# An S4 convolution and attention stack: the weights split in the first stage, and the first block of rows turned before the convolution has ended

## The chip, the cores and the metric

The kernel runs on one core of a Trainium2 chip. The metric is the device time of one execution in microseconds. Besides plain times there is one profiled execution, with a trace of every engine: TensorE (PE, with its weight loads as PEld), VectorE (DVE), ScalarE (ACT), GpSimd (POOL), SyncE (SP) and the DMA queues.

## The reference

Four layers with a residual each, over x of 2048 rows by 640 columns in float32: convolution "a", attention "b", convolution "c", attention "d". Both convolutions use the same parameters, and both attentions the same weights.

```python
def _A_ref(u, A_re, A_im, B_re, B_im, C_re, C_im, log_dt, Dskip):
    ...
    P = jnp.exp(logdA[:, :, None] * l[None, None, :])
    K = jnp.einsum("dn,dnl,dn->dl", Cc, P, dB).real
    ...
    y = irfft(rfft(pad(u)) * rfft(pad(K)))[..., :L] + u * Dskip
def _B_ref(x, wq, wk, wv, wo):
    q, k, v = heads(x @ wq), x @ wk, x @ wv      # 32 heads of 20, one k and one v
    return softmax(q @ k.T * 20 ** -0.5) @ v @ wo
x = A_u
x = x + _A_ref(_layernorm(x), ...)
x = x + _B_ref(_layernorm(x), ...)
x = x + _A_ref(_layernorm(x), ...)
x = x + _B_ref(_layernorm(x), ...)
```

## The kernel before

The stages stand one behind the other. First `kgen` makes the convolution kernel K (0 to about 340 us). `kg_tables` works out small tables on DVE and ACT; each table is cut into three bf16 parts (`cast`, `rest`), written to DRAM and read back in another layout by `send` and `send_late` into `ta`, `tb` and `tm`, all on SP's queue. Then 20 units follow: phases (`phase`, PE from `tb` and `ta`), sines (`trig`, ACT), sizes (`sizes`, PE from `tm`), exponentials, products on DVE, sums on PE. `store` puts a unit's result into the staging tile `kst`, and after each eighth unit, and after the last, `kst` goes to DRAM as `kd`. Of the load of x (`load_x`, eight DMAs) the statistics need the result from unit 5 on.

`kernel_spectra` loads `kd` back (four chunks `kts`, the fifth `ktl`, on POOL's queue) and makes the spectra `kh` of the five chunks of 128 columns. `conv_layer` then goes over the five chunks c: product with `kh`, an 8-point transform woven with other calls (`weave` puts a call at a given place between DVE instructions), and the inverse on PE for four groups g of rows, each in a PSUM bank. `residual` adds a group's result to the stream `self.x`; `turn(g)` does that and starts the inverse of group g + 2. In chunk 3 the stream itself goes through PE by an identity matmul, so that ACT only copies. Behind the last chunk stand the statistics of the rows (`stats_last`, `norm_part`).

For the attention the weights wq, wk, wv are needed as a rounded part `wh` and a rest `wl`. In layer "a" `attn_weights` makes them: six pieces, each with a copy on ACT, matmuls with the identity and its negative on PE (tile `pw`), a second copy on ACT; the pieces are woven into the last chunk's product, and both results are written to DRAM (`whd`, `wld`). In layer "c" they are only read back. `_attn` begins with `prepare(0)`: ACT normalises the first 512 rows, PE transposes them (20 transposes into tile `ptb` or `ptd`), ACT makes the rounded part `xh`, DVE the rest `xl`. Then the projections of block 0 start (tiles `pqb`, `pqd`, L1001).

On PE, ACT and DVE the order in these stages is that of the code (`manual_schedule`); in `kg_tables` also that of SP. A DMA or POOL instruction goes where the Tile framework puts it. Where pools are laid out in memory decides which tile shares its bytes with which earlier one, and a load into such bytes waits until the earlier tile's last reader is done.

Of the kernel before, what the change touches and what calls it, by code (L numbers as in the profile page):

```python
# [21 lines left out]
P = 128  # L22
# [120 lines left out]
class Net:  # L143
# [7 lines left out]
    def setup(self, ctx):  # L151
        tc, nc = self.tc, self.nc
        self.cp = ctx.enter_context(tc.tile_pool(name="cp", bufs=1))
        self.dr = ctx.enter_context(tc.tile_pool(name="dr", bufs=1, space=DRAM))
        self.ident = self.cp.tile([P, P], F32, name="ident")
        self.halfpi = self.cp.tile([P, 1], F32, name="halfpi")
        nc.vector.memset(self.halfpi, 0.5 * math.pi)
        self.xp = ctx.enter_context(tc.tile_pool(name="xp", bufs=1))
        self.x = self.xp.tile([P, 16, D], F32, name="x")
        self.mv = self.xp.tile([P, 16, 2], F32, name="mv")  # L160
        self.kd = self.dr.tile([NCH, P, 16 * DC], F32, name="kd")
        self.kh = self.dr.tile([NCH, P, 32 * DC], F32, name="kh")
# [26 lines left out]
    def kg_tables(self, pp, hs, t3, SH, ldt, aim, are_raw, bre, bim, cre, cim, ta, tb, tm):  # L189
# [49 lines left out]
        V(mn, ar, ai, ALU.min)  # L239
        T(mx, mx, 1e-37, None, ALU.max)  # L240
# [31 lines left out]
        A(u3, u2, AF.Ln, bias=1.0)  # L272
        nc.vector.tensor_copy(hs["ph"][:, 0], ph)
# [406 lines left out]
    def load_spectrum(self, c):  # L680
        A = self.cvp.tile([P, 16, 256], F32, tag="kh", bufs=2, name=f"kh{c}")
        self.nc.sync.dma_start(A.rearrange("p s d -> p (s d)"), self.kh[c])
        return A

    def kernel_spectra(self):

        nc, cv = self.nc, self.cvp

        kts = cv.tile([P, 4, 16, DC], F32, tag="wi", name="kts")
        ktl = cv.tile([P, 24, DC], F32, tag="xn", name="ktl")  # L690
        ks = [kts[:, c] for c in range(4)] + [ktl[:, 0:16]]
        dsk = ktl[0:1, 16:21]
        nc.gpsimd.dma_start(dsk.rearrange("p c d -> p (c d)"), self.ins["A_Dskip"][None, :])
        for c in range(NCH):
            nc.gpsimd.dma_start(ks[c].rearrange("p t d -> p (t d)"), self.kd[c])

        def skip(c):
            k = ks[c][0:1, 0]
            nc.vector.tensor_tensor(k, k, dsk[:, c], ALU.add)

        skip(0)
        Z = {0: self.raw(ks[0], "k0")}
        for c in range(NCH):
            if c + 1 < NCH:
                skip(c + 1)
                Z[c + 1] = self.raw(ks[c + 1], f"k{c + 1}")
            A = cv.tile([P, 16, 256], F32, tag="kh", bufs=2, name=f"kn{c}")
            weave(self.radix(Z.pop(c), A) + fft8(nc, A, self.B, self.R, -1), ())
            nc.sync.dma_start(self.kh[c], A.rearrange("p s d -> p (s d)"))

    def conv_layer(self, nm, first):
# [6 lines left out]
        with tc.manual_schedule(engines={mybir.EngineType.PE, mybir.EngineType.Activation,  # L718
# [25 lines left out]
            def new_xn(c):  # L744
                return cv.tile([P, 24, DC], F32, tag="xn", bufs=1, name=f"xn{nm}{c}")
# [18 lines left out]
            def inverse(c, g, A):  # L764
                y = self.ps1(f"y{nm}{c}{g}")
                v = A.rearrange("p s (k d) -> p s k d", k=2)
                whole = c == NCH - 2
                if whole:
                    nc.tensor.matmul(y, self.ident, stream(c, g), start=True, stop=False)
# [37 lines left out]
            for c in range(NCH):  # L807
                A = As.pop(c)
                mul = product(A, khs.pop(c)) + fft8(nc, A, B, R, +1)
                if c == NCH - 1:  # L810
                    late = sorted(late + [(1 + k, a[0]) for k, a in enumerate(pieces)]
                                  + [(3 + k, a[1]) for k, a in enumerate(pieces)], key=lambda a: a[0])
# [35 lines left out]
        turn(0)  # L848
        self.stats_base()
        self.norm_part(0, 1)  # L850
        for g in range(1, 4):
            turn(g)
        self.norm_part(1, 3)

    def attn_setup(self):
# [4 lines left out]
        self.whd = dr.tile([P, 5 * 692], F32, name="whd")  # L860
        self.wld = dr.tile([P, 5 * 692], F32, name="wld")
# [9 lines left out]
    def attn_weights(self, scr, fresh):  # L871


        nc, ins = self.nc, self.ins
        stack = ExitStack()
# [4 lines left out]
        parts = [(w.bitcast(F32), dst) for w, dst in ((wh, self.whd), (wl, self.wld))]  # L880
        if not fresh:
            for w, dst in parts:
                nc.sync.dma_start(w, dst.rearrange("p (k n) -> p k n", k=5))
            return []
        kv = wp.tile([P, 5, 52], F32, name="kv")
        nc.gpsimd.memset(kv, 0.0)
        nc.sync.dma_start(kv[:, :, 0:20], ins["B_wv"].rearrange("(k p) n -> p k n", p=P))
        nc.sync.dma_start(kv[:, :, 32:52], ins["B_wk"].rearrange("(k p) n -> p k n", p=P))
        minus = scr[:, 2816:2944]
        nc.scalar.activation(minus, self.ident, AF.Copy, scale=-1.0)  # L890
        pws = {}

        def ends(k):
            return (wh[:, k - 1, 0:D], wl[:, k - 1, 0:D]) if k else (wh[:, :, D:692], wl[:, :, D:692])

        def first(k):
            hi = ends(k)[0]
            pw = pws[k] = self.ps2(f"pw{k}")
            if k:
                src = scr[:, D * (k % 2) : D * (k % 2) + D]  # L900
                nc.sync.dma_start(src, ins["B_wq"][P * (k - 1) : P * k])
                cuts = [(pw[:, a:b], src[:, a:b], hi[:, a:b]) for a, b in ((0, 512), (512, D))]
            else:
                src = kv
                cuts = [(pw[:, 0:260].rearrange("p (k n) -> p k n", k=5), src, hi)]
            nc.scalar.activation(hi, src, AF.Copy)
            for o, a, _ in cuts:
                nc.tensor.matmul(o, self.ident, a, start=True, stop=False)
            for o, _, b in cuts:
                nc.tensor.matmul(o, minus, b.bitcast(F32), start=False, stop=True)  # L910

        def second(k):
            pw = pws.pop(k)
            src = pw[:, 0:D] if k else pw[:, 0:260].rearrange("p (k n) -> p k n", k=5)
            nc.scalar.activation(ends(k)[1], src, AF.Copy)
            if k == 5:
                for w, dst in parts:
                    nc.sync.dma_start(dst.rearrange("p (k n) -> p k n", k=5), w)

        return [(lambda k=k: first(k), lambda k=k: second(k)) for k in range(6)]  # L920
# [19 lines left out]
    def _attn(self, ctx, nm, out):  # L940
# [20 lines left out]
        with tc.tile_pool(name=f"pj{nm}", bufs=1, reuse_waits="tile") as pj:  # L961
# [5 lines left out]
            xhs, xls = {}, {}  # L967

            def prepare(nb):

                xs = []
                for i in range(4):
                    t = 4 * nb + i
                    x = pj.tile([P, D], F32, tag="x", bufs=4, name=f"x{nb}{i}")
                    nc.scalar.activation(x, self.x[:, TAUS[t]], AF.Identity, scale=self.rs[:, t : t + 1],
                                         bias=self.nmr[:, t : t + 1])
                    xs.append(x)
                xh = xhs[nb] = pj.tile([P, 5, 512], F32R, tag="xh", bufs=2, name=f"xh{nb}")
                xl = xls[nb] = pj.tile([P, 5, 512], F32R, tag="xl", bufs=2, name=f"xl{nb}")
                for k0, n in ((0, 2), (2, 2), (4, 1)):  # L980
                    pt = self.ps2(f"pt{nm}{nb}{k0}")
                    for k in range(n):
                        for i in range(4):
                            nc.tensor.transpose(pt[:, 512 * k + 128 * i : 512 * k + 128 * i + 128],
                                                xs[i][:, 128 * (k0 + k) : 128 * (k0 + k) + 128], self.ident)
                    self.split(xh[:, k0 : k0 + n], xl[:, k0 : k0 + n],
                               pt[:, 0 : 512 * n].rearrange("p (k c) -> p k c", k=n), act=True)

            def project(nb):
                cols = slice(512 * nb, 512 * nb + 512)  # L990
                xh, xl = xhs.pop(nb), xls.pop(nb)
                pn = None
                late = []
                for m in (5, 0, 1, 2, 3, 4):
# [13 lines left out]
                    if m == 1 and nb < 3:  # L1008
                        prepare(nb + 1)
# [32 lines left out]
            prepare(0)  # L1042
# [290 lines left out]
```

## Time and profile before

| | us |
|---|---|
| median of 3 runs (lowest, highest) | 3069.56 (3068.69, 3069.82) |
| profiled execution | 3071.17 |
| its span, first to last instruction | 3069.4 |
| PE busy in it | 2874.8 (94%) |
| ACT busy | 2428.3 (79%) |
| DVE busy | 1404.4 (46%) |
| POOL busy | 41.5 (1%) |

A row of the timeline gives a start, a duration, the engine, the line of the program, the operation with its tiles (out<-in), how many instructions of the kind follow one another (xN), and in brackets how long the engine had been idle before and what ended that. A row of a window gives the busy time of each engine in a stretch, the granted clock of PE, the share of time in which the DMA engines were busy, and GB/s.

### The profile page before, as it was taken

How to read it: one execution, taken by the hardware profiler on the slowest of the kernel's cores; microseconds unless marked ns; L12 is line 12 of the kernel's file. 1: busy time of each engine (PE TensorE's matmuls, PEld its weight loads, DVE VectorE, ACT ScalarE, POOL GpSimd, SP SyncE). 2: the span in 40 equal slices, each digit the busy share in tenths (PEclk: the TensorE clock that was granted, in tenths of full speed). 3: DMA queues.
4: the chain of work that ended last, by engine and by line, in shares of the span. 5: the costliest groups of instructions: out<-in, count | busy, mean ns of one | idle time of the engine just before them, and what ended most of it. 6: DMA issues, size and time to landing. Idle time of an engine off the chain costs nothing. (4 is left out here: it accounts for less than half of the span.)

```text
span 3069.4 us, 52317 instructions
## 1 busy us (share of the span) xinstructions
PE 2874.8 (94%) x21696; PEld 1362.8 (44%) x21696; DVE 1404.4 (46%) x1793; ACT 2428.3 (79%) x2910; POOL 41.5 (1%) x113
## 2 busy tenths in 40 slices
PE   2888898989899999999999989798999999999999
PEld 0555887867323323333233479673223333333233
DVE  7888799972122232232222399922122222222223
ACT  5777343353899999999999633446999999999997
POOL 0000000000100000000000000000000000000000
PEclk9999999989999999999999999899999999999999
DMA  6010551123300010000100210132000100100100
GB/s 143 18 29 17 177 220 56 38 83 131 112 24 25 22 28 22 24 25 22 27 23 24 112 55 28 50 125 79 23 22 25 39 27 24 39 25 21 45 19 22
DMA packets 72177, 158.82 MB, mean 52 GB/s; under 512 B 21509, under 2 KB 27653, under 8 KB 67797
## 3 DMA queue, kind: packets, MB, share of 16 engines
q1 hardware_dynamic: 65880, 137.70, 14.9%
q0 software_dynamic: 4080, 16.67, 1.5%
q8 instruction: 175, 2.87, 0.4%
q10 hardware_dynamic: 1968, 0.98, 0.1%
q14 instruction: 74, 0.60, 0.1%
HBM read 95.22 MB, written 48.04 MB: 47 GB/s over the span
## 5 line engine op out<-in xcount | busy, mean ns | idle before, releaser
L1134 ACT ACTIVATE pt<-scb 128x1024 f32<-128x1024 f32 x1024 | 942.2, 1115 | 7.5 <-PE scb L1130 5.8
L1134 ACT ACTIVATE pt<-scd 128x1024 f32<-128x1024 f32 x1024 | 942.2, 1118 | 7.0 <-PE scd L1130 5.5
L1144 PE MATMUL pod<-pt,vt 128*32 128x512 f32 x4096 | 546.9, 606 | 4.4 <-DVE on L1161 0.8
L1144 PE MATMUL pob<-pt,vt 128*32 128x512 f32 x4096 | 546.9, 606 | 4.3
L1130 PE MATMUL scb<-qpb,kt 62*128 62x512 f32 x2048 | 386.0, 451 | 6.2 <-PEq L1079 5.8
L1130 PE MATMUL scd<-qpd,kt 62*128 62x512 f32 x2048 | 385.8, 451 | 5.8 <-PEq L1079 5.5
L1130 PEld LDWEIGHTS scd<-qpd,kt 62*128 62x128 f32 x2048 | 166.1, 185 | 402.0 <-ACT pt L1134 392.3
L1130 PEld LDWEIGHTS scb<-qpb,kt 62*128 62x128 f32 x2048 | 165.9, 185 | 402.1 <-ACT pt L1134 392.6
L1192 DVE TENSOR_TENSOR x<-pyd,x 128x320 f32<-128x320 f32 x146 | 71.7, 491 | 561.0 <-PE pyd L1204 561.0
L1192 DVE TENSOR_TENSOR x<-pyb,x 128x320 f32<-128x320 f32 x146 | 71.7, 491 | 547.7 <-PE pyb L1204 547.7
L1164 DVE RECIPROCAL rc<-rc 128x512 f32<-128x512 f32 x62 | 207.9, 3353 | 2.1
L1144 PEld LDWEIGHTS pob<-pt,vt 128*32 128x32 f32 x4096 | 80.7, 108 | 178.3 <-issue 160.3
L1144 PEld LDWEIGHTS pod<-pt,vt 128*32 128x32 f32 x4096 | 80.6, 108 | 177.7 <-issue 159.7
L421 PE MATMUL pk<-s,m 128*64 128x32 f32 x1280 | 130.8, 295 | 13.3 <-DVE s L412 13.3
L421 PE MATMUL pk<-c,e1r 128*64 128x32 f32 x1280 | 132.1, 297 | 11.4 <-DVE c L411 11.2
L421 PEld LDWEIGHTS pk<-c,e1r 128*64 128x64 f32 x1280 | 105.3, 221 | 79.6 <-issue 52.2
L579 PE MATMUL za<-xna,wf 128*128 128x256 f32 x512 | 113.0, 383 | 2.7 <-ACT xna L733 2.7
L421 PEld LDWEIGHTS pk<-s,m 128*64 128x64 f32 x1280 | 108.1, 226 | 15.9 <-DVE s L412 15.9
L579 PE MATMUL zc<-xnc,wf 128*128 128x256 f32 x512 | 111.5, 379 | 2.7 <-ACT xnc L733 2.7
L581 ACT ACTIVATE Aa<-za 128x1024 f32<-128x1024 f32 x16 | 16.4, 1023 | 118.3 <-PE za L579 116.9
L581 ACT ACTIVATE Ac<-zc 128x1024 f32<-128x1024 f32 x16 | 16.4, 1024 | 113.7 <-PE zc L579 113.7
L579 PEld LDWEIGHTS za<-xna,wf 128*128 128x128 f32 x512 | 98.0, 192 | 16.7 <-ACT xna L733 3.3
(308 smaller groups left out, 3272.9 us busy)
## 6 DMA issues: line engine op xcount, KB each, us to landing
kh<-kh SPq DMA_DIRECT2D x10, 2048.0 KB
kh<-kn SPq DMA_DIRECT2D x5, 2048.0 KB
qhd<-qh SPq DMA_DIRECT2D x40, 256.0 KB
qld<-ql SPq DMA_DIRECT2D x40, 256.0 KB
qpb<-qhd SPq DMA_DIRECT2D x256, 40.0 KB
qpd<-qhd SPq DMA_DIRECT2D x256, 40.0 KB
ot<-on SPq DMA_DIRECT2D x216, 40.0 KB
wf<-in_c_wf POOLq DMA_DIRECT2D x16, 512.0 KB, 7.9
```

What stands on the lines that cost most here:

```text
L421: nc.tensor.matmul(PK[u][64 * par : 64 * par + 64, 32 * d : 32 * d + 32], e[u][:, d, par], c[u][:, d, par], start=first, stop=not first)
L579: nc.tensor.matmul(zv[:, :, c, kk], self.wf[:, t + 4 * h, j, c, kk], x, start=(n == 0), stop=(n == 3))
L581: nc.scalar.activation(A.rearrange("p (o s) d -> p o s d", o=2)[:, :, 2 * t : 2 * t + 2], z.rearrange("p (c o e) -> p o c e", c=2, o=2), A ...
L1130: nc.tensor.matmul(sc[:, 512 * par : 512 * par + 512], kt[rows, 128 * t : 128 * t + 128], qps[nb, hg, pr][rows], start=True, stop=True)
L1134: nc.scalar.activation(pt, sc, AF.Exp, scale=SCALE)
L1144: nc.tensor.matmul(po[32 * j : 32 * j + 32], vt[:, t], pts[step, j // 2][:, 512 * (j % 2) : 512 * (j % 2) + 512], start=(t == 0), stop=(t ...
L1164: nc.vector.reciprocal(rc, rc)
L1192: nc.vector.tensor_tensor(xh, py, xh, ALU.add)
```

## The change

It has three parts.

**The weights.** `split_weights` is called in `kg_tables`. POOL clears a part of `self.x`, which holds no data yet and serves as scratch, copies one element of `mn` into it (so that the loads wait for `mn`) and loads wq, wv and wk there by three DMAs of its own queue. `finish()` stands behind the two logarithms: ACT copies all 128 x 3460 elements to the rounded part, POOL subtracts to get the rest, and two DMAs of POOL's queue write `whd` and `wld`. `attn_weights` now only reads them back, in both layers.

**The pools.** The tiles B, R, `kh`, `kn`, `ktl` and `xn` lie in a second pool `cvq`, which is closed before the end of the convolution. The tiles `x`, `xh`, `xl` of the projections lie in a pool `pj0` beside the weights.

**The end of the convolution.** In the last chunk the stream goes through PE too (`begin`, four identity matmuls into four PSUM banks at place 3 of the weave), the inverses of the four groups follow one another, and ACT copies the results (L792). `rows_normal` and `rows_turn` take the place of `prepare`; for block 0 they are called in the convolution's end, ahead of `norm_part(1, 3)`.

```diff
@@ kg_tables
         V(mn, ar, ai, ALU.min)
+        finish = self.split_weights(mn[0:1, 0, 0:1])
...
         A(u3, u2, AF.Ln, bias=1.0)
+        finish()
@@ conv_setup
-        self.B = self.cvp.tile([P, 16, 256], F32, name="B")
-        self.R = self.cvp.tile([P, 8, 256], F32, name="R")
+        self.cvt = ExitStack()
+        self.cvq = self.cvt.enter_context(tc.tile_pool(name="cvq", bufs=1, reuse_waits="tile"))
+        self.B = self.cvq.tile([P, 16, 256], F32, name="B")
+        self.R = self.cvq.tile([P, 8, 256], F32, name="R")
@@ kernel_spectra
         kts = cv.tile([P, 4, 16, DC], F32, tag="wi", name="kts")
-        ktl = cv.tile([P, 24, DC], F32, tag="xn", name="ktl")
+        ktl = self.cvq.tile([P, 24, DC], F32, tag="xn", name="ktl")
@@ conv_layer
             def residual(c, g, y):
-                if c == NCH - 2:
+                if c >= NCH - 2:
                     nc.scalar.activation(stream(c, g), y, AF.Copy)
...
                 if c == NCH - 1:
-                    late = sorted(late + [(1 + k, a[0]) for k, a in enumerate(pieces)]
-                                  + [(3 + k, a[1]) for k, a in enumerate(pieces)], key=lambda a: a[0])
+                    def begin():
+                        both = self.ps2(f"y{nm}l")
+                        ends.extend([self.ps1(f"y{nm}{c}{g}") for g in range(2)]
+                                    + [both[:, 0:512], both[:, 512:1024]])
+                        for g in range(4):
+                            nc.tensor.matmul(ends[g], self.ident, stream(c, g), start=True, stop=False)
+                    late.append((3, begin))
                 weave(mul, late)
...
+                if c == NCH - 1:
+                    for g in range(4):
+                        inverse(c, g, A, ends[g])
+                    self.cvt.close()
+                    self.attn_rows()
+                    break
...
-                        pieces = self.attn_weights(scr, nm == "a")
+                        self.attn_weights()
...
-        turn(0)
-        self.stats_base()
-        self.norm_part(0, 1)
-        for g in range(1, 4):
-            turn(g)
-        self.norm_part(1, 3)
+            residual(c, 0, ends[0])
+            self.stats_base()
+            self.norm_part(0, 1)
+            residual(c, 1, ends[1])
+            xs = self.rows_normal(0)
+            for g in range(2, 4):
+                residual(c, g, ends[g])
+            self.rows_turn(0, xs)
+            self.norm_part(1, 3)
@@ split_weights (new)
+        flat = self.x.rearrange("p t d -> p (t d)")
+        raw, hi = (flat[:, i : i + 3460].rearrange("p (k n) -> p k n", k=5) for i in (0, 3460))
+        nc.gpsimd.memset(raw[:, :, D:692], 0.0)
+        nc.gpsimd.tensor_copy(raw[0:1, 0, 0:1], after)
+        for name, c0, n in (("B_wq", 0, D), ("B_wv", D, 20), ("B_wk", D + 32, 20)):
+            nc.gpsimd.dma_start(raw[:, :, c0 : c0 + n], ins[name].rearrange("(k p) n -> p k n", p=P))
+        def finish():
+            nc.scalar.activation(hi.bitcast(F32R), raw, AF.Copy)
+            nc.gpsimd.tensor_tensor(raw.bitcast(F32R), raw, hi, ALU.subtract)
+            for dst, w in ((self.whd, hi), (self.wld, raw)):
+                nc.gpsimd.dma_start(dst, w.rearrange("p k n -> p (k n)"))
@@ attn_weights
+        for w, src in ((wh, self.whd), (wl, self.wld)):
+            nc.sync.dma_start(w.bitcast(F32), src.rearrange("p (k n) -> p k n", k=5))
```

The order shows three places. The first is SP's queue in `kg_tables`, in the kernel before; `hdare`, `hph` and `hlw` are tables, `tm` and `ta` their layouts that PE reads, and the names behind "waits" are semaphores (DMASW those of POOL's DMAs, DMAHW those of the other queues' DMAs).

```order
L210 DMA hdare<-hare 128x1920 [waits DMAHW6_49,Activation_49]
L218 DMA ta<-hph 16x640 [waits DMAHW7_49,DVE_49]
L218 DMA ta<-hph 16x640 [waits DMAHW0_49,DVE_49]
L218 DMA ta<-hph 16x640 [waits DVE_49]
L593 DMA x<-in_A_u 64x2560 [waits DMAHW2_49]
L213 DMA tm<-hdare 16x8x640 [waits DMAHW6_49,DMAHW3_49]
```

The same place in the changed kernel, and behind it POOL's new instructions there.

```order
L212 DMA hdare<-hare 128x1920 [waits Activation_49]
L220 DMA ta<-hph 16x640 [waits DMAHW5_49,DVE_49]
L220 DMA ta<-hph 16x640 [waits DMAHW6_49,DVE_49]
L220 DMA ta<-hph 16x640 [waits DMAHW7_49,DVE_49]
L599 DMA x<-in_A_u 64x2560 [waits DMASW2_49,DMASW1_49,DMASW4_49,DMASW0_49,Pool_49]
L215 DMA tm<-hdare 16x8x640 [waits DMAHW4_49,DMAHW1_49]
```

The load of x waits for the five DMAs of POOL here, the write of `wld` the last of them (the DMASW semaphores 0 to 4 belong to wq, wv, wk, whd and wld), since it fills the scratch; the loads of `tm` stand behind it in the queue, as before. On POOL:

```order
L898 MEMSET x 128x5x52
L899 COPY x<-mn 1x1 [waits DVE_49]
L901 DMA x<-in_B_wq 128x5x640 [waits Pool_49]
L901 DMA x<-in_B_wv 128x5x20 [waits DMASW0_49]
L901 DMA x<-in_B_wk 128x5x20
L905 ISA
L905 TENSOR_TENSOR x<-x 128x3460 [waits DMASW2_49,DMASW1_49,Activation_49]
L907 DMA whd<-x 128x3460
L907 DMA wld<-x 128x3460 [waits Pool_49]
L371 MEMSET c_0_306 128x32 [waits DVE_49]
```

All of these are new but the last row, which stood at this place before; it belongs to the first unit's `trig`. ISA reloads POOL's library of code.

The second place is POOL's queue where `kd` is loaded back, before and after.

```order
L693 DMA ktl<-in_A_Dskip 1x16x40 [waits DMASW0_49,DVE_49,PE_49]
L695 DMA kts<-kd 128x2048 [waits DMAHW6_49,DMAHW7_49,DMASW1_49,Pool_49]
L695 DMA kts<-kd 128x2048 [waits DMAHW1_49,DMAHW0_49,DMASW2_49]
L695 DMA kts<-kd 128x2048 [waits DMAHW3_49,DMAHW2_49,DMASW3_49]
L695 DMA kts<-kd 128x2048 [waits DMAHW5_49,DMAHW4_49,DMASW4_49]
L695 DMA ktl<-kd 128x2048 [waits DMAHW6_49,DMAHW1_49,DMAHW7_49,DMAHW0_49,DMASW5_49]
```

In the changed kernel:

```order
L699 DMA ktl<-in_A_Dskip 1x16x40 [waits DVE_49,DMASW5_49,PE_49,Activation_49]
L701 DMA kts<-kd 128x2048 [waits DMAHW3_49,DMAHW4_49,DMAHW2_49,DMAHW5_49,DMAHW1_49,DMAHW6_49,DMAHW0_49,DMAHW7_49,DMASW6_49,Activation_49]
L701 DMA kts<-kd 128x2048 [waits DMASW7_49]
L701 DMA kts<-kd 128x2048 [waits DMASW0_49]
L701 DMA kts<-kd 128x2048 [waits DMASW1_49]
L701 DMA ktl<-kd 128x2048 [waits DMASW2_49]
```

With B and R in another pool, `kts` now lies at byte 59360 of each partition, where `kst` lay (before: 83936, beside it). So the first load of `kts` waits for all eight queues, the four last writes of `kd` from `kst` among them, where before only the fifth chunk's load did, which needs them as data.

The third place is ACT at the end of convolution "a" (tiles `ya` and `yal` are the inverse's results, `pw` the split's, `xh` the rounded part of the turned rows). Before:

```order
L915 ACTIVATE wl<-pw_4279 128x640
L915 ACTIVATE wl<-pw_4288 128x640
L915 ACTIVATE wl<-pw_4297 128x640
L658 ACTIVATE sq_4392<-ve_4391 128x4
L975 ACTIVATE x_4496<-x,nmrna,rsna 128x640
L658 ACTIVATE sq_4455<-ve_4454 128x12
L975 ACTIVATE x_4498<-x,nmrna,rsna 128x640
```

In the changed kernel:

```order
L792 ACTIVATE x<-ya_4269 128x4x128
L664 ACTIVATE sq_4377<-ve_4376 128x4
L792 ACTIVATE x<-ya_4270 128x4x128
L933 ACTIVATE x_4401<-x,nmrna,rsna 128x640
L933 ACTIVATE x_4403<-x,nmrna,rsna 128x640
L933 ACTIVATE x_4405<-x,nmrna,rsna 128x640
L933 ACTIVATE x_4407<-x,nmrna,rsna 128x640
L792 ACTIVATE x<-yal 128x4x128 x2
L887 ACTIVATE xh_4429<-pt_4431 128x1024
```

The copies of the weights are gone, the last chunk's residuals are ACT's, and the four normalisations of block 0 (L933, before L975) stand ahead of the last two residuals and of the statistics of the other rows (the `sq` of 128x12, behind the three `xh`).

More of the change, by code (lines that the diff above doesn't have):

```diff
@@ L160, in setup @@
         self.mv = self.xp.tile([P, 16, 2], F32, name="mv")
+        self.whd = self.dr.tile([P, 5 * 692], F32, name="whd")
+        self.wld = self.dr.tile([P, 5 * 692], F32, name="wld")
         self.kd = self.dr.tile([NCH, P, 16 * DC], F32, name="kd")
@@ L744, in new_xn @@
             def new_xn(c):
-                return cv.tile([P, 24, DC], F32, tag="xn", bufs=1, name=f"xn{nm}{c}")
+                return self.cvq.tile([P, 24, DC], F32, tag="xn", bufs=1, name=f"xn{nm}{c}")
             def m(a, c_):
@@ L879, in attn_weights @@
         self.wqs = stack, wh, wl
[L880 to L920, printed above, removed]
+        for w, src in ((wh, self.whd), (wl, self.wld)):
+            nc.sync.dma_start(w.bitcast(F32), src.rearrange("p (k n) -> p k n", k=5))
@@ new lines, in attn_rows, with rows_normal @@
+    def attn_rows(self):
+        stack = self.wqs[0]
+        self.pj0 = stack.enter_context(self.tc.tile_pool(name="pj0", bufs=1, side="right", reuse_waits="tile"))
+        self.xhs, self.xls = {}, {}
+    def rows_normal(self, nb):
+        xs = []
+        for i in range(4):
+            t = 4 * nb + i
+            x = self.pj0.tile([P, D], F32, tag="x", bufs=4, name=f"x{nb}{i}")
+            self.nc.scalar.activation(x, self.x[:, TAUS[t]], AF.Identity, scale=self.rs[:, t : t + 1],
+                                      bias=self.nmr[:, t : t + 1])
+            xs.append(x)
+        return xs
@@ L966, in _attn @@
             nrm = pj.tile([64, 4], F32, name="nrm")
[L967 to L987, printed above, removed]
             def project(nb):
                 cols = slice(512 * nb, 512 * nb + 512)
-                xh, xl = xhs.pop(nb), xls.pop(nb)
+                xh, xl = self.xhs.pop(nb), self.xls.pop(nb)
                 pn = None
```

35 lines of the change are left out of this document (24 added, 11 removed).

## The prediction

> **What bounds the kernel now.** I read the page first: busy times, the strip of 40 slices, and the granted clock.
>
> ```profile
> PE 2874.8 (94%) x21696; PEld 1362.8 (44%) x21696; DVE 1404.4 (46%) x1793; ACT 2428.3 (79%) x2910; POOL 41.5 (1%) x113
> PE   2888898989899999999999989798999999999999
> ```
>
> PE is busy 94% of the time, and the slices in which it is not lie at the front and at the seams between stages (slices of 77 us: the first, and the ones near 660 and 1980 us). The change touches three such places and no steady loop, so each is worked out by itself: the front (S), the reload of the convolution kernel (K) and the seams of both convolutions (G). The forecast is S + K - G against the profiled execution of 3071.17 us (span 3069.4, 1.8 us around it), which stands 1.6 us above the median of 3069.56; a difference of the two executions is carried to the median unchanged. A measurement of this kernel can tell about 0.2%, 6.1 us, from no change.
>
> **The front, S.** I read the timeline of the first 60 us and its list of waits.
>
> ```profile
> 17.00 0.82 DVE L239 TENSOR_TENSOR mn<-ar,ai 128x640 f32<-128x640 f32 x1
> 32.33 0.72 ACT L272 ACTIVATE u<-u 128x640 f32<-128x640 f32 x1
> 37.20 0.74 ACT L203 ACTIVATE hare<-resare 128x640 bf16<-128x640 f32 x1 [4.15 <-DVE resare L206]
> 42.42 0.49 DVE L290 CAST hlw<-reslw 128x640 bf16<-128x640 f32 x1
> 42.89 0.58 SPq L593 DMA_DIRECT2D x<-in_A_u  x1
> 43.57 1.47 SPq L213 DMA_DIRECT2D tm<-hdare  x3
> 45.80 1.06 ACT L375 ACTIVATE fa<-f 128x1024 f32<-128x1024 f32 x1 [5.30 <-DVE f L362]
> 52.53 1.86 PE L385 MATMUL pe<-kg,tm 48*128 48x512 bf16 x4 [5.66 <-DMA tm<-hdare]
> 57.92 1.01 PE L357 MATMUL ph<-kg,ta 96*128 96x512 bf16 x2 [2.67 <-DVE f L362]
> PE pe L385 <- DMA tm<-hdare: 5.7, 1, 5.7
> 90.00:120.00 30.00, 26.86 (x297) 16.80 (x294) 23.22 (x20) 22.39 (x23) 0.62 (x4) 1.00 0.01 2
> ```
>
> PE's first sizes start at 52.53, 9 us after SP issues `tm<-hdare`, and PE has waited 5.66 us for it. The rest of the unit loop follows PE's order behind that instruction. From 90 to 120 us PE is busy 26.86 of 30 us, so a later start is hardly made up in the loop and passes on in full.
>
> In the changed kernel SP stands at the x load, which was issued at 42.89, until `wld` has landed. That time is a chain. `mn` is ready at 17.8, and the three loads follow; wq is 1.64 MB.
>
> ```profile
> 644.01 0.33 SPq L918 DMA_DIRECT2D whd<-wh  x1
> 646.53 0.33 SPq L918 DMA_DIRECT2D wld<-wl  x1
> 652.00:654.00 2.00, 2.00 (x21) 2.00 (x20) 1.66 (x10) 0.20 (x1) 0.53 (x1) 1.00 0.91 281
> 654.00:656.00 2.00, 2.00 (x21) 2.00 (x20) 1.67 (x10) 0.00 (x0) 0.00 (x0) 1.00 0.18 63
> 649.73 2.79 POOL L952 MEMSET kt<- 1x1536 f32 x2
> 356.87 0.53 POOL L695 DMA_DIRECT2D ktl<-kd  x1 [16.13 <-DMA kd<-kst]
> ```
>
> At the 281 GB/s of the window from 652, wq takes 5.8 us, 8 with the issue and latency, or up to 12 beside the loads of x; wv and wk come after it in small pieces, so all have landed by 26 to 33. ACT's copy cannot start before the logarithm at 32.33 + 0.72 = 33.05 has ended, which is about when the loads are in. Its 3460 elements, by 0.74 us for 640 and 1.06 for 1024 (0.83 ns for each element more), take 3.1: it ends at 36.2. ACT was idle for 4.15 us before `hare` at 37.20, so this copy costs nothing by itself; were that cover gone, `hare` would be up to 3.1 us late.
>
> POOL's subtraction has no like in the trace. Its nearest rows are the memsets: 2.79 us for two of 1536, 0.91 ns an element. One pass at that pace is 3.1 us, three (two operands and a result) are 9.4; I take two, 6.2, which ends at 42.4. The reload of POOL's library (the ISA row) stands ahead of the wait for ACT and lies beside it. The Trainium skill's "GPSIMD Engine Reference", section "Elementwise — side-by-side cycle accounting", gives 4497 ns for a tensor_tensor of 2048 float32 elements; an estimate from it for 3460 is 7.6 us, and the forecast by it would be 1.4 us higher.
>
> The two writes then take 2 x 0.53 to issue (the row of `ktl`, also on POOL). Before, the same two writes of 1.77 MB went out at 644.01 and 646.53, ran at 281 GB/s to 654 and were done in the stretch of 63 GB/s, near 654.5: 10.5 us. On POOL's queue with loads just ended I take 11.5, so `wld` lands at 42.4 + 1.1 + 11.5 = 55.0, and SP comes free 12.1 us after 42.89. S = 12. Its bounds: one pass and writes at 10.5 with no second issue on the path give 50.3, S = 7; three passes, wk landing 3 us later than ACT is free and writes of 13 give 63, S = 20. The queue behind the waiting SP holds the three `tm<-hdare`, the three `tm<-hlw` and all later `ta` and `tm` rows; PE waits for the first of them, ACT's exponentials and DVE's products for PE. POOL's own memsets for the first units stand behind the subtraction, but each is 0.2 us and the sines that need them wait for nothing later than SP does.
>
> **The reload, K.** The timeline and windows around the last store of `kd`:
>
> ```profile
> 338.62 14.82 SPq L441 DMA_DIRECT2D kd<-kst  x4
> 338.63 2.11 POOL L695 DMA_DIRECT2D kts<-kd  x4
> 344.12 8.09 PE L550 MATMUL zk<-kts,wf 128*128 128x128 f32 x46 [6.18 <-DMA kts<-kd]
> 343.00:344.00 1.00, 0.00 (x0) 0.00 (x0) 0.00 (x0) 0.00 (x0) 0.00 (x0) 1.00 0.97 362
> 354.00:355.00 1.00, 1.00 (x12) 1.00 (x11) 0.00 (x0) 0.74 (x1) 0.00 (x0) 1.00 0.93 145
> ```
>
> Before, the four loads of `kts` (4.2 MB) start at 338.63 beside the four stores of the fifth chunk (1.05 MB in 256-byte pieces), and PE starts on the first at 344.12, 5.5 us later. The stores land at 356.87, when `ktl` is released. Now the first load waits for them. Alone the stores need not share: at 354, where little else runs, the queues move 145 GB/s, and 1.05 MB at that rate takes 7.2 us; with 2 us to start and to report they land at 347.9. The first load then runs alone, which I put at 0.4 us better than beside the stores. K = 347.9 - 338.6 - 0.4 = 9. At the 362 GB/s of 343 they would land after 2.9 + 1.5 us, K = 4; were they as slow as before, 356.87 - 338.63 - 0.4, K = 17.8. Behind the held load on POOL stand the other `kts` loads; PE, and through it all of `kernel_spectra`, waits for the first. Nothing else is late there, and the chunks that follow are paced by PE and DVE, so K passes on.
>
> **The seams, G.** The end of convolution "a", with the split's matmuls (tile `pw`) from the view by tile, then that of "c", which had no split:
>
> ```profile
> L910 PE MATMUL pw<-wh,xnas x22: 272/383/595, 634.1 to 645.5; 128*128 128x512 f32 x10, 128*128 128x128 f32 x10, 128*128 128x260 f32 x2
> 641.26 1.28 DVE L100 TENSOR_TENSOR Aa<-B 128x512 f32<-128x512 f32 x2
> 645.60 14.46 PE L776 MATMUL ya<-Aa,wi 128*128 128x128 f32 x128
> 668.28 2.95 DVE L869 TENSOR_TENSOR xl<-ptb,xh 128x1024 fp32r<-128x1024 f32 x3 [3.35 <-ACT xh L866]
> 669.56 0.67 PE L1001 MATMUL pqb<-xh,wh 128*52 128x512 f32 x1 [1.09 <-DVE xl L869]
> 675.12 0.39 PE L1001 MATMUL pqb<-xh,wh 128*128 128x512 f32 x1
> 672.00:674.00 2.00, 2.00 (x6) 0.95 (x5) 0.00 (x0) 1.03 (x2) 0.00 (x0) 0.50 0.00 0
> 1965.68 1.28 DVE L100 TENSOR_TENSOR Ac<-B 128x512 f32<-128x512 f32 x2
> 1966.51 16.73 PE L776 MATMUL yc<-Ac,wi 128*128 128x128 f32 x128 [8.38 <-DVE Ac L100]
> 1983.28 0.69 DVE L787 TENSOR_TENSOR x<-yc,x 128x512 f32<-128x512 f32 x1 [1.17 <-PE yc L776]
> 1984.01 1.40 DVE L630 BATCH_NORM_STATS2 sl<-x 128x6 f32<-128x256 f32 x4
> 1985.33 0.36 DVE L632 BATCH_NORM_AGGREGATE mvbc<-sl 128x2 f32<-128x6 f32 x4
> 1992.73 0.43 PE L1001 MATMUL pqd<-xh,wh 128*52 128x512 f32 x1 [1.09 <-DVE xl L869]
> 1996.25 0.39 PE L1001 MATMUL pqd<-xh,wh 128*128 128x512 f32 x1
> ```
>
> In "a" the inverse waits for the `pw` matmuls. Without them it starts when the first half of `Aa` is ready, 0.83 us after 641.26 as in "c" (1965.68 to 1966.51): at 642.1, but after idle time, so at the 16.73 us of "c" and not at 14.46. It ends at 658.8 (before: 645.60 + 14.46 = 660.06). Then the order has, in sequence, the last two residuals on ACT (some 0.6, as DVE's 0.69), the statistics of two groups (2 x (1.40 + 0.36) = 3.5), and the first `xl` on DVE, 1.28 us before PE may start (668.28 to 669.56): 5.4, with gaps 5.6. The transposes lie beside that. The projection starts at 664.4 instead of 669.56: 5.1 us. It also runs while PE has been busy for longer; before, its first 15 matmuls took 5.56 us (669.56 to 675.12) at a granted clock of 0.50, in "c" 3.52 (1992.73 to 1996.25): 2.0 us. G_a = 7, between 3 (no warmer clock, a longer chain) and 9.
>
> In "c" nothing ahead of the inverse changes: the four identity matmuls of `begin` lie in the weave, in the 8.38 us in which PE waits there. 1965.68 + 0.83 + 16.73 gives 1983.2, and 5.6 more is 1988.8, against 1992.73: G_c = 4, between 2 and 6. G = 11, between 5 and 15. What is late next are the rows of block 1, whose `norm_part` now stands behind `xl`; they are needed only after two column groups of the projection, 3.5 us each, and are hidden.
>
> The sum: 12 + 9 - 11 = +10 us, so 3081.2 for the profiled execution and 3079.6 for the median. With the three terms' middle values uncertain by about 4, 3 and 3 us, this case's own range is 3073 to 3087.
>
> **The rivals.** *POOL is kept from its subtraction.* DVE works on the tables, often with two operands from memory, until `hlw` is done near 43 (the row at 42.42); if POOL gets its turn only then, it ends at 43 + 6.2, `wld` lands at 61.8 and S = 19: 3086.6. The Trainium skill's "SBUF — State Buffer", section "Who interferes with whom", has DVE and GpSimd share a port pair as an exclusive lock, the second one blocked; no run here shows it, since before POOL computes nothing but memsets. A first call after the library's reload that lasts some us would do the same. Against it: DVE's instructions are 0.5 to 0.8 us long, with gaps between. 0.14.
>
> *The stores are slow by themselves.* 145 GB/s at 354 is a rate with the loads nearly gone, so it speaks for 7 us, but SP's issue of the four lasts 14.82 in the row above. If the stores take as long alone, K = 17.8: 3088.4. 0.10.
>
> *A quick front.* One pass on POOL, S = 7: 3074.6. For it: the memsets' pace. 0.12.
>
> *The held queue is not on the path (the other side).* If `wld` has landed before SP reaches the load of x, or the 5.66 us that PE waits there are slack that the unit loop makes up, then S = 0, and 9 - 11 leaves -2: 3067.6. It decides at S + K = G: with K = 9 and G = 11 the write of `wld` must have landed by 45. For it: the loop's PE is idle 3 of each 30 us, so some of S can come back. Against it: the row in which PE waits 5.7 us for just this table, and the 10.5 us that the two writes alone take behind a copy that cannot end before 36.2. 0.12.
>
> *The seam of "a" gains nothing*, because the projection is held by something else, such as the load of `wh` and `wl` or the copy of `ob`; G = 4: 3086.6. Against it: those loads are issued a chunk earlier. 0.04.
>
> **How the numbers follow.** The forecast has 0.48, the rivals 0.14, 0.10, 0.12, 0.12 and 0.04. The median is predicted at 3079.6. The range reaches from 3071 to 3092: it holds the forecast, the slow rivals with 3 to 5 us to spare and the quick front, and leaves out most of the rival on the other side. Faster by over 0.2% (below 3063.4) needs that rival with G at its top, and gets 0.05. Within 0.2% (to 3075.7) come the rest of it, 0.07, half of the quick front, 0.06, and the low end of the forecast, 0.07: 0.20. Slower by over 0.2% is the rest, 0.75.
>
> **What would show it.** In the changed profile SP's load of x (L599) should be issued near 55, PE's first sizes (the line of `pe`) start near 64.6 and wait over 15 us for `tm`; POOL's subtraction should take near 6 us. `kd<-kst` should land near 9 us after its issue, and PE's first `zk` start 14 to 15 us after it (5.5 before). The first `pqb` should follow the end of the inverse by 5.6 us (9.5 before) and the first `pqd` likewise. The prediction is wrong if PE's first sizes start before 56, if the first `zk` follows the stores' issue within 8 us, or if the projections start no earlier against the inverse.

## The result and the profile after

The changed kernel takes 3083.14 us (median of 6 runs, 3081.25 to 3084.04) against 3070.22 (6 runs, 3068.69 to 3072.17) before: a ratio of 1.0042, 95% interval 1.0032 to 1.0052. It is 12.9 us slower. The prediction was 3079.6, in a range of 3071 to 3092. The profiled execution has a span of 3082.1 us, 12.7 more than before.

The page's busy times, as shown of before:

```profile
PE 2867.5 (93%) x21668; PEld 1357.3 (44%) x21668; DVE 1407.3 (46%) x1785; ACT 2427.5 (79%) x2906; POOL 53.7 (2%) x120
```

PE has 7.3 us less to do (the split's matmuls are gone, some identity matmuls are new) and POOL 12.2 more; the loss is all in waits.

The front, from the timeline of the first 70 us of the changed kernel:

```profile
34.75 3.09 ACT L904 ACTIVATE x<-x 128x3460 fp32r<-128x3460 f32 x1 [1.57 <-DMA x<-in_B_wk]
37.92 7.85 POOL L905 TENSOR_TENSOR x<-x 128x3460 fp32r<-128x3460 f32 x1 [8.41 <-ACT x L904]
38.48 8.43 DVE L286 TENSOR_SCALAR lw<-lw,ldt 128x128 f32<-128x128 f32 x5
46.31 0.55 POOL L907 DMA_DIRECT2D wld<-x  x1
48.36 0.34 SPq L212 DMA_DIRECT2D hdare<-hare  x1
56.79 0.51 SPq L599 DMA_DIRECT2D x<-in_A_u  x1
57.21 1.22 DVE L179 TENSOR_SCALAR r<-ph 128x1024 bf16<-128x1024 f32 x1 [6.47 <-DMA hdare<-hare]
57.39 1.49 SPq L215 DMA_DIRECT2D tm<-hdare  x3
59.84 1.01 PE L361 MATMUL ph<-kg,ta 96*128 96x512 bf16 x2 [24.23 <-DVE f L366]
66.50 1.86 PE L389 MATMUL pe<-kg,tm 48*128 48x512 bf16 x4 [5.65 <-DMA tm<-hdare]
```

SP's load of x goes out at 56.79 (42.89 before), `tm<-hdare` behind it, and PE's first sizes start at 66.50 for 52.53: S = 14.0. Two rows were not foreseen. DVE's five small instructions (L286) last 8.43 us, 1.07 before, while POOL subtracts; so `hdare` is sent at 48.36 and not at 40.53. And DVE's first `r`, which waits for `hdare`, starts 8.9 us after that DMA's issue, 2.7 before. PE is held on two paths at once: its phases (`ph`), which stand ahead of the sizes and wait for DVE's `r` and `f`, start at 59.84 for 45.86, also 14.0 us late.

The view of that line, with minimum, median and longest duration in ns, shows that a single one of the five took it all:

```profile
L286 DVE TENSOR_SCALAR lw<-lw,ldt x5: 273/472/7373, 38.5 to 46.6; 128x128 f32<-128x128 f32 x5
```

And the window of the writes (its last two columns are the DMA engines' busy share and GB/s) shows the DMA engines nearly full:

```profile
46.00:57.00 11.00, 0.00 (x0) 0.00 (x0) 4.60 (x10) 0.74 (x1) 1.20 (x6) 1.00 0.92 372
```

The reload of `kd`:

```profile
352.65 4.38 SPq L445 DMA_DIRECT2D kd<-kst  x4
361.54 2.16 POOL L701 DMA_DIRECT2D kts<-kd  x4 [8.46 <-DMA kd<-kst]
366.71 8.46 PE L556 MATMUL zk<-kts,wf 128*128 128x128 f32 x52 [14.73 <-DMA kts<-kd]
```

The stores land 8.9 us after their issue, then the loads start; `zk` follows the stores by 14.06 us, before by 5.50: K = 8.6. The two seams:

```profile
663.61 1.29 DVE L100 TENSOR_TENSOR Aa<-B 128x512 f32<-128x512 f32 x2
664.35 9.47 PE L783 MATMUL ya<-Aa,wi 128*128 128x128 f32 x64 [4.93 <-DVE Aa L100]
673.66 7.31 PE L783 MATMUL yal<-Aa,wi 128*128 128x128 f32 x64
681.01 1.09 ACT L792 ACTIVATE x<-yal 128x512 f32<-128x512 f32 x2 [2.89 <-PE yal L783]
686.06 0.67 PE L1007 MATMUL pqb<-xh,wh 128*52 128x512 f32 x1 [2.90 <-DVE xl L890]
690.96 0.40 PE L1007 MATMUL pqb<-xh,wh 128*128 128x512 f32 x1
1981.87 9.48 PE L783 MATMUL yc<-Ac,wi 128*128 128x128 f32 x64 [4.92 <-DVE Ac L100]
2003.59 0.67 PE L1007 MATMUL pqd<-xh,wh 128*52 128x512 f32 x1 [2.90 <-DVE xl L890]
2008.53 0.39 PE L1007 MATMUL pqd<-xh,wh 128*128 128x512 f32 x1
```

In "a" the shift against the kernel before falls from 22.35 us (`Aa`, 663.61 against 641.26) to 16.50 at the first projection (686.06 against 669.56) and 15.84 at its first wide product (690.96 against 675.12). In "c" it falls from 15.36 (1981.87 against 1966.51) to 10.86 (2003.59 against 1992.73), and rises again to 12.28 at 2008.53. At the end it is 12.7: G = 14.0 + 8.6 - 12.7 = 9.9 us.

### The profile page after: what moved, and what is told of

Its sections match the earlier page's. It is cut to its first block, busy times and chain, and to the rows that moved or that the text cites. A ratio compares the mean times of both kernels' runs of the same rounds, so it can differ in the third digit from the quotient of the medians.

```text
span 3082.1 us, 52262 instructions
## 1 busy us (share of the span) xinstructions
PE 2867.5 (93%) x21668; PEld 1357.3 (44%) x21668; DVE 1407.3 (46%) x1785; ACT 2427.5 (79%) x2906; POOL 53.7 (2%) x120
## 3 DMA queue, kind: packets, MB, share of 16 engines
q1 hardware_dynamic: 63848, 135.96, 14.7%
## 5 line engine op out<-in xcount | busy, mean ns | idle before, releaser
L425 PE MATMUL pk<-c,e1r 128*64 128x32 f32 x1280 | 132.1, 297 | 11.5 <-DVE c L415 11.2
L1209 PE MATMUL pyb<-wo,ot 128*32 128x320 f32 x1168 | 105.3, 432 | 0.0
```

What stands on the lines that cost most here:

```text
L425: nc.tensor.matmul(PK[u][64 * par : 64 * par + 64, 32 * d : 32 * d + 32], e[u][:, d, par], c[u][:, d, par], start=first, stop=not first)
L1209: nc.tensor.matmul(py[j : j + m], o[:, 128 * i + j : 128 * i + j + m], w[:, 320 * half : 320 * half + 320], start=start, stop=stop)
```

## The experiments

All comparisons are with runs of the kernel before beside them, 3069.4 to 3069.7 us in the median. Ten further kernels ran.

**The three causes in the front.** The next four take away one of them or make one alone; no run has the held queue alone.

*Scratch outside x.*

```diff
-        raw, hi = (flat[:, i : i + 3460].rearrange("p (k n) -> p k n", k=5) for i in (0, 3460))
+        raw, hi = (pp.tile([P, 5, 692], F32, name=n) for n in ("wraw", "whi"))
```

> The changed kernel, with the scratch of the weights split in bytes of its own in the tables' pool and not in x, so that SP no longer waits for wld; subtraction and writes stay as they are. If the held SP queue is what sets S, the first sizes on PE come 6 us earlier (60.5 for 66.5; what is left is 7.8 us by which DVE was late) and the time is about 3077. If DVE's lateness and the traffic of the two writes, beside which hdare lands, set it, SP is free and hdare still lands near 57: first sizes at 65 to 67, time 3082 to 3083.

It took 3081.88 us, ratio 1.0042 (1.0028 to 1.0056). Its timeline:

```profile
48.35 0.34 SPq L212 DMA_DIRECT2D hdare<-hare  x1
55.78 1.27 SPq L215 DMA_DIRECT2D tm<-hdare  x3
55.85 1.23 DVE L179 TENSOR_SCALAR r<-ph 128x1024 bf16<-128x1024 f32 x1 [5.11 <-DMA hdare<-hare]
63.79 1.86 PE L389 MATMUL pe<-kg,tm 48*128 48x512 bf16 x4 [4.29 <-DMA tm<-hdare]
```

SP no longer waits for `wld`, and still the sizes come at 63.79: S = 11.3. The wait that the prediction named is real, but taking it away returns only 2.7 of 14.0 us, since `hdare` lands near 55.8 by itself. In the time no gain can be told: the ratio to the kernel before is 1.0042, as for the changed kernel.

*The subtraction alone,* in the kernel before.

```diff
+        A(hi.bitcast(F32R), raw, AF.Copy)
+        nc.gpsimd.tensor_tensor(raw.bitcast(F32R), raw, hi, ALU.subtract)
```

> The kernel before, with only ACT's copy and POOL's subtraction of 128 x 3460 elements of a cleared tile at that place in the tables: no loads, no writes, no wait on SP. If the subtraction by itself stops DVE, L286's row (here a few lines further on) takes 8 us and the first sizes come 7.5 to 8 us later than before (60.3 for 52.5): time 3078. If only SP's wait and the writes cost, the time is that of before, 3070.

3076.56 us, ratio 1.0026 (1.0017 to 1.0036). Its timeline:

```profile
36.27 7.64 POOL L276 TENSOR_TENSOR wraw<-wraw,whi 128x3460 fp32r<-128x3460 f32 x1 [32.55 <-ACT whi L275]
36.50 8.08 DVE L206 TENSOR_TENSOR resare<-are,hare 128x640 f32<-128x640 f32 x1
60.05 1.86 PE L389 MATMUL pe<-kg,tm 48*128 48x512 bf16 x4 [5.76 <-DMA tm<-hdare]
```

A DVE subtraction of 640 elements, 0.82 us in the kernel before, lasts 8.08: it ends 0.7 us after POOL's, so for all but its own 0.8 us it stood still. Not the instruction that the expectation named was caught, but the one that came next when POOL had begun. First sizes 7.5 us late.

*The writes alone,* in the kernel before: `od` and `pd` are DRAM tiles like `whd` and `wld`.

```diff
+        nc.gpsimd.tensor_copy(hi[0:1, 0:1], res["are"][0:1, 0, 0:1])
+        nc.gpsimd.dma_start(od, hi)
+        nc.gpsimd.dma_start(pd, raw)
```

> The kernel before, with only two writes of 128 x 3460 cleared elements to DRAM on POOL's queue, issued at about 37.6 us, 3 us ahead of hdare: no subtraction, no ACT copy, no wait on SP. If the traffic of such writes delays the small tables, DVE's first r, which waits for hdare, starts at 46 to 49 (43.2 before) and the first sizes at 56 to 58 (52.5): time 3074 to 3076. If the two only share bandwidth without cost, first sizes stay within 1 us and the time at 3070.

3076.4 us, ratio 1.0023 (1.0013 to 1.0032). Its timeline:

```profile
39.34 0.56 POOL L286 DMA_DIRECT2D pd<-wraw  x1
40.75 0.34 SPq L210 DMA_DIRECT2D hdare<-hare  x1
51.31 1.23 DVE L177 TENSOR_SCALAR r<-ph 128x1024 bf16<-128x1024 f32 x1 [7.95 <-DMA hdare<-hare]
59.16 1.86 PE L393 MATMUL pe<-kg,tm 48*128 48x512 bf16 x4 [4.21 <-DMA tm<-hdare]
```

The window of the writes:

```profile
40.00:51.00 11.00, 0.00 (x0) 0.00 (x0) 3.22 (x5) 0.72 (x1) 0.24 (x4) 1.00 1.00 382
```

`hdare` is 0.5 MB and needs 10.6 us from issue to use instead of 2.7, behind 3.5 MB that were issued 1.4 to 2.2 us earlier. First sizes 6.6 us late.

*Without the subtraction.*

```diff
-            nc.gpsimd.tensor_tensor(raw.bitcast(F32R), raw, hi, ALU.subtract)
```

> The changed kernel without POOL's subtraction (so the rest of the weights holds the weights themselves): loads, ACT's copy, both writes and SP's wait stay. If DVE stood still because POOL held the memory port, the five small DVE instructions (L286) take 1.1 us again (8.4 in the changed kernel), the writes go out 7.9 us earlier, and first sizes come near 58.5; time about 3075. If DVE's 8.4 us had another cause, DVE stays late and the time falls by less than 3 us.

With these weights the attention takes its other branch, so the total (5636 us) tells nothing; only the front is read.

```profile
35.17 0.68 POOL L906 DMA_DIRECT2D wld<-x  x1 [5.51 <-DMA x<-in_B_wk]
38.62 1.07 DVE L286 TENSOR_SCALAR lw<-lw,ldt 128x128 f32<-128x128 f32 x5
41.75 0.49 SPq L599 DMA_DIRECT2D x<-in_A_u  x1
46.33 0.38 SPq L212 DMA_DIRECT2D hdare<-hare  x1
62.05 1.86 PE L389 MATMUL pe<-kg,tm 48*128 48x512 bf16 x4 [3.29 <-DMA tm<-hdare]
```

DVE is free (1.07 again). But SP's order is another one here: a load of x goes out at 41.75, ahead of `hdare` and of the table before it (`ta<-hdthr`, at 42.33 for 35.70 in the changed kernel). SP's list of waits says what held it:

```profile
SPq L599 <- DMA wld<-x: 7.0, 1, 7.0
```

So the write of `wld`, earlier by 11 us, holds the queue earlier too, and `hdare` goes out at 46.33, 5.8 us later than in the kernel before. First sizes at 62.05, not 58.5: S = 9.5. This run therefore shows that DVE's standstill goes with the subtraction, and not what the subtraction costs by itself. The three are not terms of a sum: the subtraction and the writes cost 7.5 and 6.6 alone and 11.3 together, and the wait on SP makes it 14.0.

**The reload.** Two ways to part `kts` from `kst`:

```diff
+        below = self.spectrum("below")
         kts = cv.tile([P, 4, 16, DC], F32, tag="wi", name="kts")
...
+        nc.sync.dma_start(below[0:1, 15, 255:256], self.ins["A_Dskip"][None, 0:1])
```

> The changed kernel, with kts moved off the bytes of kst (the spectra tiles, tag A, take its place in the pool). If the reload term K is real (8.4 us between the last stores of kd and the first zk, beyond what it was before), the first zk follows the stores by 5.5 to 6 us again (14.1 in the changed kernel) and the time falls by 8 to 9, to about 3074.5. If the wait at the reload had been given back later, the time stays at 3083.

and B and R back in the first pool:

```diff
-        self.B = self.cvq.tile([P, 16, 256], F32, name="B")
+        self.B = self.cvp.tile([P, 16, 256], F32, name="B")
```

> The changed kernel, with B and R in the first pool again, so that kts lies where it did in the kernel before, clear of kst; the rest of the second pool stays. The reload should cost less than the 8.6 us. In the run with kts apart the loads were issued 0.5 us behind the stores (before: together) and zk followed by 8.7 us instead of 5.5. If that half microsecond decides, zk follows by 8 to 9 us here too, and the time is 3077 to 3078; if it was the other layout (an extra DMA on SP, the spectra tiles below), it follows by 5.5 to 6 and the time is 3074.

3077.58 us (ratio 1.0027, 1.0016 to 1.0038) and 3076.79 (1.0024, 1.0014 to 1.0033). Timeline of the second:

```profile
352.67 13.15 SPq L445 DMA_DIRECT2D kd<-kst  x4
353.20 2.16 POOL L701 DMA_DIRECT2D kts<-kd  x4
360.81 1.36 PEld L556 LDWEIGHTS zk<-kts,wf 128*128 128x128 f32 x6 [8.95 <-DMA kts<-kd]
```

The loads no longer wait for the stores, and `zk` follows these by 8.1 us (8.7 in the first), not 14.1 and not 5.5. The overlap of the two tiles was worth 5 to 6 us of the 8.6. The rest goes with 0.5 us: the loads are issued that much behind the stores (`ktl<-in_A_Dskip`, ahead of them on POOL, now waits for ACT too). That the lag costs it is inferred from all kernels together: those with no lag (before, and the two with one part of the front alone) have 5.3 to 5.5 us, those with 0.53 to 0.54 have 8.1 to 8.8. But each kernel with the lag also has the second pool `cvq`, and none without it has. No run changed the lag alone, so the other 3 us stay unexplained.

**The seams.** The old split, with the new seams (B and R lie in the first pool, and in "a" the last residual is a DVE add without the identity matmuls):

```diff
-        finish = self.split_weights(mn[0:1, 0, 0:1])
...
-                        self.attn_weights()
+                        pieces = self.attn_weights(scr, nm == "a")
```

> The front and the weights split of the kernel before (woven into the last chunk of convolution a), with the new seams: rows of block 0 normalised and turned early, all inverses in a row. In a the residual is a DVE add (the identity matmuls would come on top of the split's), in c it goes through PE. If the gain of the seams comes from the early rows and not from the moved split, G is 3 to 4 us at a and 4 at c, and the time 3062 to 3064. If the split's move was needed for it, a gives nothing: 3066 or more.

3066.21 us, ratio 0.9991 (0.9981 to 1.0). Its stores and loads have the half microsecond's lag (`zk` 8.8 us behind the stores, so 3.3 us lost), which the expectation left out; by the times the seams alone gain about 6.7. Its trace at the seam of "a":

```profile
645.03 1.28 DVE L100 TENSOR_TENSOR Aa<-B 128x512 f32<-128x512 f32 x2
669.74 0.44 PE L1028 MATMUL pqb<-xh,wh 128*52 128x512 f32 x1 [2.11 <-DVE xl L890]
673.26 0.39 PE L1028 MATMUL pqb<-xh,wh 128*128 128x512 f32 x1
```

From `Aa` to the first projection it gains 3.6 us on the kernel before (the changed kernel 5.9), to the first wide product 5.6 (6.5), since here the projection runs warm; in "c" it gains 3.5 to that point, the changed kernel 3.2. So the early rows bring most of G: two thirds by the times, over nine tenths in this trace. Moving the split brings 2.3 us up to the projection of "a"; how much of that stays to the end the runs do not settle.

**A version without the costs.** In the changed kernel, with B and R below:

```diff
         cast("are", are, 2)
+        self.split_hi()
...
                 phase(0, h)
+            self.split_lo()
...
+                if u == 2:
+                    self.split_out(S1[u][0:1, 0, 0, 0:1])
+                    self.load_x()
...
-                if 5 <= u < 13:
-                    self.stats(u - 5)
+                if 7 <= u < 15:
+                    self.stats(u - 7)
...
-        nc.gpsimd.dma_start(dsk.rearrange("p c d -> p (c d)"), self.ins["A_Dskip"][None, :])
         for c in range(NCH):
+            if c == NCH - 1:
+                nc.gpsimd.dma_start(dsk.rearrange("p c d -> p (c d)"), self.ins["A_Dskip"][None, :])
```

`split_hi` is ACT's copy, `split_lo` the subtraction, on DVE, `split_out` the two writes. The last lines move the load of A_Dskip behind the four `kts`, so that these no longer stand behind its waits.

> The changed kernel with all costs of the front and the reload moved where nothing waits: ACT's copy of the weights behind its last cast of a table, the subtraction on DVE behind the second phase (DVE waits 5.9 us there), the two writes on POOL behind the memsets of unit 2 (all tables are sent by then) and the x loads behind them, the statistics from unit 7 on; B and R as in the run before it, and A_Dskip loaded behind the four kts, so that those are issued ahead of the stores. By my reading S and K become 0 to 1 us and G, 9.7 us in the changed kernel, is left: first sizes at 52.5 to 53.5, zk 5.5 us behind the stores, time 3060 to 3062, faster than the kernel before. If the gain at the seams only existed because everything ran late, the time is 3070.

3056.8 us, ratio 0.9958 (0.9942 to 0.9975): 12.8 us faster than the kernel before. Its timeline:

```profile
49.58 1.86 PE L389 MATMUL pe<-kg,tm 48*128 48x512 bf16 x4 [2.29 <-DMA tm<-hdare]
49.72 3.75 DVE L911 TENSOR_TENSOR x<-x 128x3460 fp32r<-128x3460 f32 x1
327.49 2.09 POOL L705 DMA_DIRECT2D kts<-kd  x4 [6.31 <-DVE m L413]
336.33 0.51 POOL L704 DMA_DIRECT2D ktl<-in_A_Dskip  x1 [6.76 <-PE pk L425]
336.70 6.51 SPq L445 DMA_DIRECT2D kd<-kst  x4
342.79 29.46 PE L559 MATMUL zk<-kts,wf 128*128 128x128 f32 x247 [3.17 <-DVE kts L709]
```

The first sizes come 3 us earlier than in the kernel before, which neither theory had. The loads of `kts` go out 9.2 us ahead of the stores. In the kernel before, POOL's queue stands for 14.7 us at A_Dskip, which waits for PE, and only then come the loads, together with the stores:

```profile
338.04 0.51 POOL L693 DMA_DIRECT2D ktl<-in_A_Dskip  x1 [14.74 <-PE pk L421]
```

And PE stops for 3.2 us where DVE waits for A_Dskip, which now comes late. Two runs follow from this: x's loads late in the kernel before,

```diff
-                if u == 0:
+                if u == 2:
+                    for g in range(4):
+                        nc.gpsimd.tensor_copy(self.x[:, 4 * g, 0:1], S1[u][:, 0, 0, 0:1])
                     self.load_x()
```

> The kernel before, with only the eight loads of x held until unit 2 (a small copy on POOL into each of their parts) and the statistics from unit 7 on. In the version with the free front the first sizes came at 49.6, 3 us earlier than in the kernel before, and tm took 6 us from issue to use instead of 9. If this is the traffic of the x loads that is gone, first sizes come at 49 to 50 here too and the time falls by 2 to 3, to 3067. If it was something else in that version, they come at 52.5 and the time stays at 3069.6.

3065.49 us, ratio 0.9985 (0.9975 to 0.9994), and A_Dskip early in the free version:

```diff
-        dsk = ktl[0:1, 16:21]
+        dsk = self.R[0:1, 4:7].rearrange("p s d -> p (s d)")[:, 0:D]
```

> The version with free front and reload, with A_Dskip loaded into an unused corner of R ahead of the kts loads, and not behind them. There PE stopped after its first 16 matmuls of zk for 3.2 us, until DVE had A_Dskip (landed 6 us after its issue). If that wait is all that is left of the reload, zk runs on and the time falls by 3 us, to 3053 to 3054. If the DVE chain behind it sets the spectra's pace anyway, the time stays at 3057.

3052.57 us, ratio 0.994 (0.9924 to 0.9957), the fastest of all. First sizes in the timeline of the kernel with x late:

```profile
48.94 1.88 PE L385 MATMUL pe<-kg,tm 48*128 48x512 bf16 x4 [2.15 <-DMA tm<-hdare]
```

`zk` in that of the version with A_Dskip early, where PE no longer stops:

```profile
340.15 32.02 PE L559 MATMUL zk<-kts,wf 128*128 128x128 f32 x283 [0.24 <-DVE kts L709]
```

So even the kernel before lost 3.6 us at the front (48.94 for 52.53) to its own loads of x beside the small tables.

The traces also show where the 17 us of the fastest version come from, against the profile of the kernel before (19.0 in the spans). The last stores go out at 336.86 for 338.62, only 1.8 us earlier, where the kernel with x late has 3.5; so the split seems not quite free: some 1.7 us are lost in the units. The first `kh` goes out at 366.31 for 374.61, 8.3 us earlier: the reload gives 6.5. The rest, some 10.7, comes behind that, about what the seams gain.

## Why the prediction was right, and where not

Sign, size and range held; the sum of +10 came out as +12.7, and all three terms are within about 2 us: S 14.0 for 12, K 8.6 for 9, G 9.9 for 11 (G as what is left of the sum; the shifts at the two seams give 6.5 + 3.1 = 9.6).

*S: the chain was right, the claim that it alone sets S was not.* ACT's copy ended 1.6 us later than reckoned (wk landed at about 34.7, so the wait for the loads and not the logarithm decided), the subtraction took 7.85 for the 6.2 of two passes, and the writes landed about 9.9 us after both had been issued, for 11.5. The estimate of 7.6 us from the Trainium skill's "GPSIMD Engine Reference", section "Elementwise — side-by-side cycle accounting", fits the trace (7.64 to 7.91 in five kernels) better than the bounds from memsets. The step that failed is the sentence that the rest of the queue simply waits behind SP: `hdare`, which stands ahead of the held load, was itself late twice, by DVE's standstill and by the writes' traffic. Each alone costs about half of S (7.5 and 6.6), together 11.3, and SP's wait lies over them and adds only 2.7. That S came so near is partly luck: `wld` and `hdare` landed within half a microsecond of each other (56.79 and 57.21 are what they released), and only the first was in the sum. PE was to wait over 15 us for `tm` and waited 5.65 as before, since the phases ahead of it were as late.

*The rival of the shared port had the roles reversed.* It let POOL starve; POOL began first, and DVE stood still for nearly the whole subtraction, 7.1 to 7.4 us. The rule behind it, in the Trainium skill's "SBUF — State Buffer", section "Who interferes with whom" (an exclusive lock, whoever comes second is blocked), agrees with these rows. The price that was put on it did not, since most of DVE's delay lies under SP's wait.

*K: right as written.* The stores alone take 8.9 us, 9.3 reckoned from the 145 GB/s of one microsecond. What was not seen is that without the overlap some 3 us of it stay, from a cause that no run isolates.

*G: the chain was right, the clock was not.* From the inverse's end to the projection 5.1 us pass in "a" (680.97 to 686.06), 5.6 reckoned; 5.85 us are gained to that point for 5.1, and 4.5 in "c" for 3.9. But the projection was to run warmer, 2.0 us: in "a" it takes 4.90 us to the first wide product (5.56 before), in "c" 4.94 (3.52 before). So "a" gains 0.7 and "c" loses 1.4. The window of "c" shows a granted clock of 0.50, where the kernel before has 1.00 (1992.7 to 1994.5):

```profile
2003.60:2006.60 3.00, 3.00 (x7) 1.45 (x8) 2.65 (x10) 0.21 (x1) 0.00 (x0) 0.50 0.02 5
```

PE now idles 2.90 us ahead of the projection in both layers. It does so too in both layers of five runs (the scratch outside x, the two on the reload, the version without the costs and the one with A_Dskip early) and in "c" of the run with the old split, and in all these places the first seven matmuls ran at a granted clock of 0.50 to 0.54; in "a" of the run with the old split, after 2.11 us, it was 1.00. That the idle time is the cause is inferred: no run changes it alone, and in the kernel before "a" was at 0.50 after 1.09 us.

*The other side* needed S near 2; it never came near: the units gave nothing back, with 14.0 us at the first sizes and 14.0 at the last stores (352.65 for 338.62).

## What to carry to other kernels

Work moved into a quiet-looking stage must be costed on every resource that the stage's critical chain uses: here POOL's arithmetic stopped DVE, 3.5 MB of writes stood ahead of a 0.5 MB table, and a scratch tile held a queue, each behind the other, so that removing the one named first gave back a fifth. When pools are rearranged, look at which bytes a tile inherits. And the same work seems to cost 1.7 us instead of 14.0 once it stood where its engine waits anyway (a DVE gap, a queue with nothing left to send). Looking for that place also uncovered two waits of the kernel before, x's loads beside the tables and A_Dskip ahead of the reload.

## What the runs showed of the hardware

- A POOL subtraction of two tiles held DVE: one instruction of 0.27 us took 7.37 (changed kernel), one of 0.82 took 8.08 (the subtraction alone). DVE does the same subtraction of 3460 elements in 3.75 us, POOL in 7.64 to 7.91.
- With the DMA engines full (382 GB/s, share 1.00), a transfer of 0.5 MB issued 1.4 to 2.2 us behind two of 1.77 MB in another queue landed only about when these did (10.6 us from issue to use instead of 2.7).
- Loads issued 0.5 us behind stores of small pieces let PE start 8.1 to 8.8 us after the stores, loads issued with them 5.3 to 5.5; that the lag is the cause is inferred, since the layout differs too.
